# Window attention scores by tiles of 64 rows and 32 columns, q read where it was loaded, and loads cut into portions and tied to the matmuls

## The chip, the cores and the metric

One core of a Trainium2 chip runs the whole program. Its engines work side by side: PE (TensorE) multiplies matrices, DVE (VectorE) and ACT (ScalarE) do element-wise work and empty PE's result banks, POOL (GpSimd) copies and gathers, and SP (SyncE) issues most DMAs, one after the other. Each engine works through its own list of instructions in order and waits at semaphores for the others. PE writes its results to eight PSUM banks (`ps0` to `ps7`), each of 128 partitions and 512 float32 columns. PE multiplies a stationary operand, brought in by a weight load (PEld in the profile), with a moving operand that streams past it. The time is that of the device, in microseconds (us), median of several runs; lower is better.

## The reference, cut to what matters

```python
# attention, for each of 8 batches and 8 heads of 64 dimensions
s_g   = scale * q_g @ concat(k_g, k_l).T            # 32 global queries see all 32 + 512 keys
out_g = softmax(s_g) @ concat(v_g, v_l)
s_ll  = scale * q_l @ k_l.T                         # 512 local queries see keys within 32 places
s_ll  = where(abs(i - j) <= 32, s_ll, -1e9)
s_lg  = scale * q_l @ k_g.T                         # and the 32 global keys
out_l = softmax(concat(s_lg, s_ll)) @ concat(v_g, v_l)
x     = concat(out_g, out_l), heads side by side    # 8 x 544 tokens of 512 numbers
# mixture of experts: each token goes to one expert e, its own best or that of the token before it
logits = x @ w_gate                                 # 8 experts
e      = argmax(logits) or the expert of the token before, by the gate x @ w_local
out    = softmax(logits)[e] * (relu(x @ w1[e]) @ w2[e])
```

All data are float32.

## The kernel before, in words

The program has two parts. The attention fills about the first 230 us, the experts fill the rest. This case is about the attention.

A batch has four pairs of heads. One pair is one local unit (`l`): 512 queries of two heads, cut into 16 windows of 32 queries, each of which sees 128 key columns (its own window, one on either side, and the 32 global keys). Two global units (`g`), each for two pairs, compute the 32 global queries. In the function `run` the units stand in the order l, l, g, l, g, l for every batch, and one step `s` of its loop takes one unit. The step's place in the batch, `s % 6`, is called k0 to k5 below: k0, k1, k3 and k5 begin a local unit, k2 and k4 a global one.

Each step does the first half of the work for its own unit `nx` (scores, row maximum, exponent) and the second half for the unit `st` of two steps before (transposes, product with v, division by the row sums). In between, `fpiece` puts in one piece of the router's work on the finished rows: `f1` transposes a pair's output, `f2` and `f3` compute the gate's logits for a whole batch, and `f1g` and `f2g` do so for the global rows. Small router instructions on DVE are let in one at a time by `drip`.

A local unit is worked in two halves of eight windows (`hb` 0 and 1):

- `prep` copies on POOL. It spreads q of the two heads into `qbd`, where the other head's places hold zeros, and copies k with the global keys into `kx`. Both lie in rings of two buffers.
- `l_s` writes the mask into a score bank by one bf16 matmul with the identity (`idb`), and adds eight score matmuls to it. Each has 128 rows of contraction (two heads, one of them zeros) and 64 columns (32 queries of both heads), so two of them fill the bank's 128 partitions side by side.
- `l_max` takes the row maximum and subtracts it on DVE; `l_exp` is on ACT.
- `l_t` transposes the four 128 x 128 blocks of a half on PE, and ACT copies them to `pt`.
- `l_av` multiplies with v in 16 matmuls of 32 columns, four side by side, and DVE divides by the sums into `xa`, the batch's output rows.

The score banks are a ring of four, the banks for `l_av`, `g_av`, `f2`, `f2g` and a part of `f3` a ring of two (`ps_o`), and `xa` a ring of two batches. When the router has finished a batch, `f4` stores `xa` (1056 KB), `xg` and `gx` to the DRAM array `xs` through SP's list. The first `l_av` of the batch after next writes the same `xa` buffer and waits until that store has landed.

SP's list holds the loads of the attention as well: at each local step one load of q and k (`raw`, a ring of four, 528 KB) for the pair two ahead, and one of v (1040 KB, a ring of five) for the next pair. They wait only for their buffers to come free. SP waits at the head of its list, so whatever stands behind a waiting DMA waits too.

float32 matmuls appear in the profile as two records each (two passes), bf16 and fp32r ones and transposes as one.

Of the kernel before, what the change touches and what calls it, by code (L numbers as in the profile page):

```python
# [18 lines left out]
P = 128  # L19
# [16 lines left out]
NBUF = 2  # L36
# [63 lines left out]
class Attn:  # L100
    def __init__(self, tc, cst, tl, at1, at2, raw, ps, qk, qg, vw, xs):
# [13 lines left out]
        self.rs = ring(tl, [P, 2, 2, 1], F32, "rs", 3)  # L115
# [6 lines left out]
        self.pt = ring(at1, [P, 4, 2, 2, 32], F32, "pt", 4)  # L122
        self.qbd = ring(at2, [P, NW, 2, 32], F32, "qbd", NBUF)
# [4 lines left out]
        self.mask = at2.tile([P, 8, 2, 32], BF16, name="mask")  # L128
# [5 lines left out]
        self.npr = 0  # L134

    def make_mask(self):
# [8 lines left out]
        nc.vector.tensor_copy(self.mask, m0.rearrange("p (o a) k -> p o a k", o=1).broadcast_to([P, 8, 2, 32]))  # L145
        nc.vector.memset(self.mask[0:64, 0, 0, :], NEG)
        nc.vector.memset(self.mask[64:128, 7, 1, :], NEG)
# [45 lines left out]
    def prep(self, u):  # L193
# [3 lines left out]
        q = t[:, 0:SL].rearrange("p (w q) -> p w q", q=32)  # L197
        qbd, kx = u["qbd"], u["kx"] = self.qbd(), self.kx()
        k = t[:, SL:]
        kf = kx.rearrange("p m c k -> p (m c) k")  # L200
        if self.npr == 0:
            nc.scalar.copy(out=qbd[0:64, :, 0, :], in_=q[0:64])
            nc.vector.tensor_copy(qbd[64:128, :, 1, :], q[64:128])
            nc.vector.tensor_copy(kx[:, 1:8, 2, :], k[:, 32:64].rearrange("p (o k) -> p o k", o=1).broadcast_to([P, 7, 32]))
        else:
            self.cp(qbd[0:64, :, 0, :], q[0:64], [[0, NW], [0, 32]])
            self.cp(qbd[64:128, :, 1, :], q[64:128], [[0, NW], [0, 32]])
# [7 lines left out]
    def blank(self, i):  # L215
        nc = self.nc
        qbd, kx = self.qbd.t[i], self.kx.t[i]
        nc.vector.memset(qbd[0:64, :, 1, :], 0.0)
        nc.vector.memset(qbd[64:128, :, 0, :], 0.0)
        nc.vector.memset(kx[:, 0, 0], 0.0)  # L220
        nc.vector.memset(kx[:, 8, 1:3], 0.0)
# [4 lines left out]
    def l_s(self, st, hb):  # L226
        nc = self.nc
        if hb == 0:
            b, pr = st["u"]
            if pr == 0:  # L230
                self.cur[b]["xa"] = self.xa()
                self.cur[b]["xg"] = self.xg()
            st["pe"] = self.pe()
        qbd = st["qbd"]
        kf = st["kx"].rearrange("p m c k -> p (m c k)")
        sp = st["sp"] = self.bank(self.ps_s)
        mo = sp.rearrange("p t (k c) -> p t k c", c=32)[:, :, 0::3, :]
        nc.tensor.matmul(mo, self.cst.idb, self.mask[:, 4 * hb:4 * hb + 4], start=True, stop=False, skip_group_check=True)
        for t in range(4):
            for t2 in range(2):  # L240
                w = 8 * hb + 2 * t + t2
                f = 32 * (3 * (w // 2) + w % 2)
                nc.tensor.matmul(sp[64 * t2:64 * t2 + 64, t], qbd[:, w], kf[:, f:f + P], start=False, stop=True, skip_group_check=True)  # L243

    def l_max(self, st, hb):
        nc = self.nc
        mx = self.mx()
        nc.vector.tensor_reduce(out=mx, in_=st["sp"], axis=AX.X, op=ALU.max)  # L248
        self.drip()
        nc.vector.tensor_tensor(out=st["pe"][:, 4 * hb:4 * hb + 4], in0=st["sp"], in1=mx.broadcast_to([P, 4, P]), op=ALU.subtract)  # L250

    def l_exp(self, st, hb):
        pe = st["pe"][:, 4 * hb:4 * hb + 4]
        self.nc.scalar.activation(out=pe, in_=pe, func=AF.Exp, scale=SCALE)  # L254

    def l_t(self, st, hb):
        nc = self.nc
        tp = self.bank(self.ps_t)
        for i in range(4):
            nc.tensor.transpose(tp[:, i], st["pe"][:, 4 * hb + i], self.cst.idf)  # L260
        pt = self.pt()
        nc.scalar.copy(out=pt.rearrange("p i t h q -> p i (t h q)"), in_=tp)  # L262
        st["pts"] = st.get("pts", []) + [pt]

    def l_av(self, st, hb):
# [4 lines left out]
        pt = st["pts"][hb]  # L270
        o = self.ps_o()[:, 0:2 * VW].rearrange("p (g h c) -> p g h c", h=2, c=D + 1)
        for g in range(2):
            for h in range(2):
                for w4 in range(4):
                    w = 8 * hb + 4 * g + w4
                    nc.tensor.matmul(o[32 * w4:32 * w4 + 32, g, h], pt[:, 2 * g + w4 // 2, w4 % 2, h, :],  # L276
                                     v[:, w, h * (D + 1):(h + 1) * (D + 1)], start=True, stop=True, skip_group_check=True)
        rs = self.rs()
        nc.vector.tensor_scalar(out=rs, in0=o[:, :, :, D:D + 1], scalar1=1e-9, scalar2=None, op0=ALU.add)
# [3 lines left out]
        xo = c["xa"][:, 2 * hb:2 * hb + 2, 2 * D * pr:2 * D * (pr + 1)].rearrange("p g (h c) -> p g h c", c=D)  # L283
        nc.vector.tensor_tensor(out=xo, in0=o[:, :, :, 0:D], in1=rs.broadcast_to([P, 2, 2, D]), op=ALU.mult)
# [1290 lines left out]
```

## Time and profile before

| what | value |
|---|---|
| median of three runs | 690.67 us (690.36 to 690.69) |
| the profiled execution: time, span | 694.06 us, 692.3 us |
| mean granted TensorE clock | 0.995 |
| PE busy | 670.5 us, 97% of the span |
| weight loads (PEld) | 561.1 us |
| DVE busy | 426.2 us |
| ACT busy | 342.9 us |
| POOL busy | 207.7 us |
| DMA | 151.44 MB, mean 219 GB/s |

How to read it: "busy" of an engine is time in which at least one of its instructions runs. A group of instructions is named by its line in the kernel, the engine and the tiles it writes and reads (`ps<-kx,qbd` writes a PSUM bank from `kx` and `qbd`). The ends of matmuls are modelled, and consecutive ones overlap, so a matmul's duration is a latency; its cost is the distance from its start to the next start. The timeline merges equal instructions that follow one another into one row, with the start of the first.

### The profile page before, as it was taken

What the parts mean: (1) busy time and instruction counts of PE and PEld (TensorE: products, weight loads), DVE (VectorE), ACT (ScalarE), POOL (GpSimd) and SP (SyncE); (2) the same over time, 40 slices, a digit from 0 to 9 for tenths busy, and PEclk for the clock granted to TensorE, in tenths of its full rate; (3) what the DMA queues carried; (4) which work ended last, traced back from release to release, by engine and by line L of the source; (5) the groups of instructions that cost most, each with busy time, mean ns of one, the idle gap of its engine ahead of it and who ended that gap; (6) DMA issues with size and microseconds to landing.
All of it is one profiled execution on the core that took longest, in us unless ns stands there. A gap on an engine that the chain in (4) does not pass through costs nothing.

```text
span 692.3 us, 18408 instructions
## 1 busy us (share of the span) xinstructions
PE 670.5 (97%) x7253; PEld 561.1 (81%) x7253; DVE 426.2 (62%) x1050; ACT 342.9 (50%) x614; POOL 207.7 (30%) x342
## 2 busy tenths in 40 slices
PE   9999999999989899998998999999999999999995
PEld 7777777777767787897887988889898889888994
DVE  7878677688887777995517535335354516255572
ACT  4555556555455674653326625344444325255553
POOL 7634334343674301033013303040404020133023
PEclk9999999999999999999999999999999999999999
DMA  8956957866856497777418647337475417265673
GB/s 318 405 220 233 346 193 309 310 248 231 299 196 273 147 356 243 260 243 245 174 60 308 232 149 239 102 117 235 145 225 191 140 61 231 66 222 193 212 270 103
DMA packets 43011, 151.44 MB, mean 219 GB/s; under 512 B 7965, under 2 KB 9245, under 8 KB 38688
## 3 DMA queue, kind: packets, MB, share of 16 engines
q1 hardware_dynamic: 35536, 126.92, 51.6%
q0 software_dynamic: 6960, 21.90, 9.5%
q8 instruction: 77, 1.26, 0.7%
q14 instruction: 150, 1.23, 0.6%
q10 hardware_dynamic: 288, 0.13, 0.1%
HBM read 130.55 MB, written 19.69 MB: 217 GB/s over the span
## 4 chain that ended last, share of the span: by engine, by line
PE 60%; DVE 3%; issue 1%; ACT 0%; POOL 0%; POOLq 0%; DVEq 0%; ACTq 0%
PE ps L1267 29%; PE ps L1256 27%; PE ps L1210 3%; DVE wq L1165 1%; DVE wp L1165 1%; PE ps L1004 0%; PE ps L1379 0%; DVE xl L1165 0%; DVE xT L994 0%; POOL xa L1196 0%; DVE xT L996 0%; POOLq L1427 0%; DVE wp L1213 0%; PE ps L276 0%; DVE wq L1371 0%
## 5 line engine op out<-in xcount | busy, mean ns | idle before, releaser
L1273 POOL DMA_INDIRECT out_dram<-y,tk x39 | 40.4, 1036 | 317.6 <-ACT y L1272 246.3
L1267 PE MATMUL ps<-wp,wq 128*128 128x512 f32 x504 | 128.4, 402 | 1.0 <-ACT wq L1370 1.0
L1267 PEld LDWEIGHTS ps<-wp,wq 128*128 128x128 f32 x504 | 93.5, 190 | 21.1 <-ACT wq L1370 1.2
L1256 PE MATMUL ps<-wp,wp 128*128 128x256 f32 (+5 forms) x672 | 109.3, 322 | 0.2 <-issue 0.2
L1256 PEld LDWEIGHTS ps<-wp,wp 128*128 128x128 f32 x672 | 103.6, 188 | 5.3 <-issue 0.4
L1259 DVE SCALAR_TENSOR_TENSOR wq<-ps,wq 128x256 fp32r<-128x256 f32 (+5 forms) x80 | 41.7, 525 | 72.8 <-ACT wq L1258 62.6
L1213 DVE TENSOR_TENSOR wp<-ps,wp 128x512 fp32r<-128x512 f32 x40 | 27.5, 691 | 78.9 <-ACT wp L1212 78.8
L1258 ACT ACTIVATE wq<-ps 128x256 fp32r<-128x256 f32 (+5 forms) x80 | 37.3, 468 | 78.3 <-PE ps L1256 68.8
L191 POOL TENSOR_SCALAR_AFFINE_SELECT qbd<-raw 64x512 f32<-64x512 f32 x62 | 44.4, 716 | 103.3 <-PE ps L243 85.5
L243 PE MATMUL ps<-kx,qbd 128*64 128x128 f32 x1024 | 71.3, 280 | 0.2 <-issue 0.2
L1272 ACT ACTIVATE y<-ps,pp 128x512 f32<-128x512 f32 x39 | 26.9, 690 | 77.7 <-PE ps L1267 71.1
L243 PEld LDWEIGHTS ps<-kx,qbd 128*64 128x64 f32 x1024 | 55.1, 137 | 12.2 <-issue 7.8
L248 DVE TENSOR_REDUCE mx<-ps 128x4 f32<-128x512 f32 x64 | 43.9, 687 | 29.9 <-PE ps L243 29.9
L1165 DVE TENSOR_TENSOR wp<-raw,wp 128x1024 fp32r<-128x1024 f32 x47 | 57.0, 1217 | 2.8 <-ACT wp L1155 2.8
L254 ACT ACTIVATE pe<-pe 128x512 f32<-128x512 f32 x64 | 40.7, 637 | 31.7 <-DVE pe L250 31.7
L1196 POOL DMA_INDIRECT xa<-xs,idx x42 | 50.9, 1212 | 17.1 <-issue 9.4
L1155 ACT CAST wp<-raw 128x1024 fp32r<-128x1024 f32 x49 | 50.8, 1047 | 0.8 <-ACT hh L1258 0.5
L1212 ACT CAST wp<-ps 128x512 fp32r<-128x512 f32 x40 | 23.4, 590 | 53.9 <-PE ps L1210 53.3
L250 DVE TENSOR_TENSOR pe<-ps,mx 128x512 f32<-128x512 f32 x64 | 44.0, 688 | 1.6
L276 PEld LDWEIGHTS ps<-v,pt 128*32 128x32 f32 x2048 | 33.4, 110 | 13.1 <-issue 7.3
L276 PE MATMUL ps<-v,pt 128*32 128x65 f32 x2048 | 42.8, 222 | 1.1 <-issue 0.4
L262 ACT COPY pt<-ps 128x512 f32<-128x512 f32 x64 | 34.9, 610 | 17.6 <-PE ps L260 17.6
(280 smaller groups left out, 1183.3 us busy)
## 6 DMA issues: line engine op xcount, KB each, us to landing
raw<-in_w_dram SPq DMA_DIRECT2D x78, 512.0 KB, 4.1
v<-in_vw_dram SPq DMA_DIRECT2D x32, 1040.0 KB, 9.8
raw<-in_qk_dram SPq DMA_DIRECT2D x32, 528.0 KB, 8.2
xa<-in_w_dram SPq DMA_DIRECT2D x26, 512.0 KB, 5.2
xT<-in_w_dram SPq DMA_DIRECT2D x20, 512.0 KB, 3.5
xs<-xa SPq DMA_DIRECT2D x8, 1056.0 KB, 4.9
qgb<-in_qg_dram SPq DMA_DIRECT2D x8, 128.0 KB, 3.5
xa<-xs,idx POOLq DMA_INDIRECT x42
```

The lines of the kernel that those rows point to most:

```text
L191: self.nc.gpsimd.affine_select(out=out, in_=in_, pattern=pat, compare_op=ALU.is_ge, fill=0.0, base=0, channel_multiplier=0)
L243: nc.tensor.matmul(sp[64 * t2:64 * t2 + 64, t], qbd[:, w], kf[:, f:f + P], start=False, stop=True, skip_group_check=True)
L248: nc.vector.tensor_reduce(out=mx, in_=st["sp"], axis=AX.X, op=ALU.max)
L250: nc.vector.tensor_tensor(out=st["pe"][:, 4 * hb:4 * hb + 4], in0=st["sp"], in1=mx.broadcast_to([P, 4, P]), op=ALU.subtract)
L254: self.nc.scalar.activation(out=pe, in_=pe, func=AF.Exp, scale=SCALE)
L276: nc.tensor.matmul(o[32 * w4:32 * w4 + 32, g, h], pt[:, 2 * g + w4 // 2, w4 % 2, h, :], v[:, w, h * (D + 1):(h + 1) * (D + 1)], start=True ...
L1155: nc.scalar.copy(out=hi, in_=raw)
L1165: (nc.gpsimd if pool else nc.vector).tensor_tensor(out=lo, in0=raw, in1=hi.bitcast(F32), op=ALU.subtract)
L1196: self.nc.gpsimd.indirect_dma_start(out=self.xr[j] if k == "early" else self.xr4[:, j], out_offset=None, in_=src, in_offset=bass.IndirectO ...
L1256: nc.tensor.matmul(ph, a[:, dc, fs], b_[:, dc, n0:n1], start=(n == 0), stop=(n == 11))
L1259: nc.vector.scalar_tensor_tensor(out=hl[:, fc, n0:n1], in0=ph, scalar=0.0, in1=hh[:, fc, n0:n1].bitcast(F32), op0=ALU.max, op1=ALU.subtract)
L1267: nc.tensor.matmul(py, a[:, fc, js], b_[:, fs], start=(fc == 0 and k == 0), stop=(fc == 7 and k == 2))
```

## The change

Scores are now computed for each head apart, with 64 rows of contraction and 32 columns. `qbd` is gone: q is read where the load put it, rows 0 to 63 for the first head and 64 to 127 for the second. A score bank now belongs to one head (`h` 0 or 1) and holds all 16 windows: window `4*t + w4` in partitions `32*w4` and block `t`. A unit's two masks are written one after the other, right behind the transposes (`l_m`); then come all 32 score matmuls (`l_s`), alternating between the heads, and only then the two halves of the rest, which are now heads. `g_s` makes two matmuls of 32 columns where it made one of 64. `l_av` keeps its 16 matmuls for each half, and each of its two writes to `xa` now covers all 512 queries of one head.

Loads are issued by `feed`, twice in each step and each time a part: half of a v tile (520 KB), or one q-and-k tile. `get` adds to each a wait for the matmul that was last put into PE's list (`gate`). `f4` stores `xa` in two DMAs.

```diff
-        self.qbd = ring(at2, [P, NW, 2, 32], F32, "qbd", NBUF)
...
-            self.cp(qbd[0:64, :, 0, :], q[0:64], [[0, NW], [0, 32]])
-            self.cp(qbd[64:128, :, 1, :], q[64:128], [[0, NW], [0, 32]])
...
+    def get(self, out, in_):
+        d = self.nc.sync.dma_start(out, in_)
+        if self.gate is not None:
+            self.tc.add_manual_dep(d.ins, self.gate.ins.name, mybir.DependencyInfo(mybir.DependencyClass.Sync, mybir.DependencyReason.DATA), reason="pace")
...
+    def feed(self, s, hf):
+        b, k = divmod(s, 6)
+        if k < 3:
+            if b == 0 and k < 2 and hf == 0:
+                self.load(0, 2 + k)
+            self.loadv(b, 1 + k, hf)
+            return
+        b += 1
+        if b == B:
+            return
+        if k == 4:
+            self.loadv(b, 0, hf)
+        else:
+            self.load(b, (k - 3) + hf)
+            if (k, hf) == (3, 0):
+                self.load_g(b)
...
+    def l_m(self, st):
...
+        st["sps"] = [self.bank(self.ps_s) for _ in range(2)]
+        for sp in st["sps"]:
+            mo = sp.rearrange("p t (k c) -> p t k c", c=32)[:, :, 0::3, :]
+            nc.tensor.matmul(mo, self.cst.idb, self.mask, start=True, stop=False, skip_group_check=True)
+
+    def l_s(self, st):
+        nc = self.nc
+        q, kf = st["q"], st["kx"].rearrange("p m c k -> p (m c k)")
         for t in range(4):
-            for t2 in range(2):
-                w = 8 * hb + 2 * t + t2
+            for w4 in range(4):
+                w = 4 * t + w4
                 f = 32 * (3 * (w // 2) + w % 2)
-                nc.tensor.matmul(sp[64 * t2:64 * t2 + 64, t], qbd[:, w], kf[:, f:f + P], start=False, stop=True, skip_group_check=True)
+                for h in range(2):
+                    d = slice(64 * h, 64 * h + 64)
+                    self.gate = nc.tensor.matmul(st["sps"][h][32 * w4:32 * w4 + 32, t], q[d, 32 * w:32 * w + 32], kf[d, f:f + P],
+                                                 start=False, stop=True, skip_group_check=True)
...
-        nc.sync.dma_start(self.xs[r0:r0 + 4 * P].rearrange("(t p) r -> p t r", p=P), xa)
+        for t in range(0, 4, 2):
+            nc.sync.dma_start(self.xs[r0 + t * P:r0 + t * P + 2 * P].rearrange("(t p) r -> p t r", p=P), xa[:, t:t + 2])
...
             if nl:
-                self.l_s(nx, 0)
+                self.l_m(nx)
+                self.l_s(nx)
                 self.l_max(nx, 0)
             else:
                 self.g_s(nx)
                 self.g_max(nx)
+            self.feed(s, 0)
             fpiece()
             if sl:
                 self.l_av(st, 0)
             if nl:
                 self.l_exp(nx, 0)
-                self.l_s(nx, 1)
                 self.l_max(nx, 1)
             fpiece()
...
+            self.feed(s, 1)
```

How the change moves instructions shows at three places. The first is PE's list at step k5 of the first batch, where a local unit begins and another ends. `ps_65` and `ps_66` are score banks, `ps_69` and `ps_70` banks of `l_av`. Before:

```order
L260 MATMUL ps_67<-idf,pe_139 128x128 x4
L260 MATMUL ps_68<-idf,pe_139 128x128 x4
L238 LDWEIGHTS idb
L238 MATMUL ps_65<-mask,idb 128x4x2x32
L243 MATMUL ps_65<-kx_147,qbd_145 64x128 x8
L276 MATMUL ps_69<-v_134,pt_140 32x65 x16
L238 LDWEIGHTS idb
L238 MATMUL ps_66<-mask,idb 128x4x2x32
L243 MATMUL ps_66<-kx_147,qbd_145 64x128 x8
L276 MATMUL ps_70<-v_134,pt_141 32x65 x16
```

The same place in the changed kernel, up to the first two score matmuls:

```order
L280 MATMUL ps_67<-idf,pe_139 128x128 x4
L280 MATMUL ps_68<-idf,pe_139 128x128 x4
L251 LDWEIGHTS idb
L251 MATMUL ps_65<-mask,idb 128x4x2x32
L251 LDWEIGHTS idb
L251 MATMUL ps_66<-mask,idb 128x4x2x32
L262 MATMUL ps_65<-kx_145,raw_80 32x128
L262 MATMUL ps_66<-kx_145,raw_80 32x128
```

The last two rows come sixteen times over, and then the two groups of `l_av` follow each other without scores between them.

The second place is SP's list at step k2 of the third batch, where the first batch's rows are stored. Before, with the semaphores that each row waits for (DMAHW is an earlier DMA):

```order
L178 DMA raw_80<-in_qk_dram 128x1056 [waits DMAHW3_49,Pool_49]
L188 DMA v_132<-in_vw_dram 128x2080 [waits DMAHW4_49,PE_49]
L413 DMA xs<-xa_108 128x4x528 [waits DMAHW5_49,DVE_49]
L417 DMA xs<-xg_110 32x2x64 [waits DMAHW6_49]
L417 DMA xs<-xg_110 32x2x64 [waits DMAHW7_49]
```

and in the changed kernel:

```order
L173 DMA v_132<-in_vw_dram 128x1040 [waits DMAHW6_49,PE_49]
L173 DMA v_132<-in_vw_dram 128x1040 [waits DMAHW7_49,PE_49]
L173 DMA v_133<-in_vw_dram 128x1040 [waits DMAHW0_49,PE_49]
L434 DMA xs<-xa_108 128x2x528 [waits DMAHW1_49,DVE_49]
L434 DMA xs<-xa_108 128x2x528 [waits DMAHW2_49]
L438 DMA xs<-xg_110 32x2x64 [waits DMAHW3_49]
```

The store had the v load of step k1 ahead of it; now it has half a v load of step k2 ahead of it, whose wait on PE is for the last matmul of `g_s` in that same step.

The third place is DVE's list at the same step, where `l_av` of the third batch's first pair writes into `xa_108`, in the changed kernel:

```order
L324 TENSOR_REDUCE m_128<-ps_64 128x1 [waits PE_49]
L324 TENSOR_REDUCE m_128<-ps_65 128x1 [waits PE_49]
L326 TENSOR_SCALAR nb_126<-m_128 128x1 [waits DVE_49]
L397 COPY gsb_115<-ps_69 128x32 [waits PE_49]
L297 TENSOR_SCALAR rs_122<-ps_70 128x4 [waits PE_49]
L299 RECIPROCAL rs_122<-rs_122 128x4 [waits DVE_49]
L302 TENSOR_TENSOR xa_108<-ps_70,rs_122 128x4x64 [waits DMAHW2_49,DMAHW1_49,DVE_49]
```

Its last row waits for both halves of the store; its counterpart in the kernel before (line 284) stands at the same place in DVE's list and waits for the one store.

More of the change, by code (lines that the diff above doesn't have):

```diff
@@ L134, in __init__ @@
         self.npr = 0
+        self.gate = None
     def make_mask(self):
@@ L224, in bank @@
         return r().rearrange("p (t k) -> p t k", k=P)
-    def l_s(self, st, hb):
+    def l_m(self, st):
         nc = self.nc
[L228 to L238, printed above, removed]
+        b, pr = st["u"]
+        if pr == 0:
+            self.cur[b]["xa"] = self.xa()
+            self.cur[b]["xg"] = self.xg()
+        st["pe"] = self.pe()
+        st["sps"] = [self.bank(self.ps_s) for _ in range(2)]
+        for sp in st["sps"]:
+            mo = sp.rearrange("p t (k c) -> p t k c", c=32)[:, :, 0::3, :]
+            nc.tensor.matmul(mo, self.cst.idb, self.mask, start=True, stop=False, skip_group_check=True)
@@ L259, in l_t, with l_av @@
         for i in range(4):
[L260 removed]
+            nc.tensor.transpose(tp[:, i], st["pe"][:, 4 * h + i], self.cst.idf)
         pt = self.pt()
[L262 removed]
+        nc.scalar.copy(out=pt, in_=tp)
         st["pts"] = st.get("pts", []) + [pt]
[L265 removed]
+    def l_av(self, st, h):
         nc = self.nc
@@ L269, in l_av @@
         v = c["v"][pr]
[L270 to L277, printed above, removed]
+        pt = st["pts"][h]
+        o = self.ps_o()[:, 0:4 * (D + 1)].rearrange("p (t c) -> p t c", c=D + 1)
+        for t in range(4):
+            for w4 in range(4):
+                self.gate = nc.tensor.matmul(o[32 * w4:32 * w4 + 32, t], pt[:, t, 32 * w4:32 * w4 + 32],
+                                             v[:, 4 * t + w4, h * (D + 1):(h + 1) * (D + 1)], start=True, stop=True, skip_group_check=True)
         rs = self.rs()
-        nc.vector.tensor_scalar(out=rs, in0=o[:, :, :, D:D + 1], scalar1=1e-9, scalar2=None, op0=ALU.add)
+        nc.vector.tensor_scalar(out=rs, in0=o[:, :, D:D + 1], scalar1=1e-9, scalar2=None, op0=ALU.add)
         self.drip(hold=True)
@@ L295, in g_s @@
                 k = c[("qk", pr)][:, SL:]
-                nc.tensor.matmul(sp[64 * i:64 * i + 64, 0:n1 - n0], c["qg"][:, pr], k[:, n0:n1], start=True, stop=True, skip_group_check=True)
+                for h in range(2):
+                    r = 64 * i + 32 * h
+                    self.gate = nc.tensor.matmul(sp[r:r + 32, 0:n1 - n0], c["qg"][:, pr, h], k[:, n0:n1], start=True, stop=True, skip_group_check=True)
             st["sp"].append(sp[:, 0:n1 - n0])
@@ L439, in run @@
         self.load_g(0)
-        self.loadv(*pairs[0]["u"])
+        for hf in range(2):
+            self.loadv(0, 0, hf)
         self.cst.ident()
```

66 lines of the change are left out of this document (27 added, 39 removed).

## The prediction

> **What bounds the kernel now.** I read the page's busy times first, then the busy times by stretch, one stretch for each attention batch (cut where the last scores of step k5 end), then PE's timeline of two steps, DVE's timeline of the same, and SP's.
>
> ```profile
> PE 670.5 (97%) x7253; PEld 561.1 (81%) x7253; DVE 426.2 (62%) x1050; ACT 342.9 (50%) x614; POOL 207.7 (30%) x342
> ```
> ```profile
> core 0: us, PE busy (x) PEld busy (x) DVE busy (x) ACT busy (x) POOL busy (x), PEclk, DMA share, GB/s
> 0.00:26.70 26.70, 25.11 (x414) 19.54 (x414) 21.16 (x65) 13.30 (x29) 18.78 (x70) 1.00 0.91 352
> 26.70:55.20 28.50, 28.19 (x589) 21.27 (x587) 21.86 (x81) 16.01 (x37) 11.06 (x24) 1.00 0.73 278
> 55.20:83.00 27.80, 27.80 (x591) 21.19 (x589) 21.09 (x73) 16.02 (x38) 11.07 (x24) 1.00 0.75 271
> 83.00:110.90 27.90, 27.49 (x585) 21.06 (x585) 20.81 (x69) 15.73 (x37) 11.06 (x24) 1.00 0.73 270
> 110.90:139.10 28.20, 28.20 (x601) 21.42 (x597) 21.57 (x78) 16.30 (x38) 11.06 (x24) 1.00 0.80 292
> 139.10:167.40 28.30, 27.94 (x593) 21.17 (x594) 22.40 (x83) 16.16 (x39) 11.07 (x24) 1.00 0.61 230
> 167.40:200.00 32.60, 30.79 (x616) 23.06 (x614) 27.35 (x94) 15.75 (x38) 23.13 (x45) 1.00 0.67 238
> 200.00:231.00 31.00, 29.98 (x619) 23.02 (x617) 24.12 (x81) 17.98 (x39) 13.24 (x24) 1.00 0.72 272
> ```
>
> Batches 1 to 5 (second to sixth row; batches count from 0) are PE's: it is busy for all of their 28 us. DVE is at 21 to 22 of 28, so a faster PE can win 6 to 7 us there before DVE is full. In the two last batches, where the router's work comes on top, DVE has 27.35 and 24.12 us. The experts behind 231 us are not touched, so all gain or loss lies in these eight rows. Next, PE in one local step (k5) and in steps k1 to k3:
>
> ```profile
> 118.68 0.33 PE L359 MATMUL ps<-idf,xg 128*128 128x128 f32 x1
> 118.94 0.66 PE L276 MATMUL ps<-v,pt 128*32 128x65 f32 x32
> ...
> 121.37 1.09 PE L260 MATMUL ps<-idf,pe 128*128 128x128 f32 x8
> 122.39 1.14 PE L296 MATMUL ps<-raw,qgb 128*64 128x256 f32 x8
> 123.46 0.27 PE L375 MATMUL ps<-xgT,wgg 128*32 128x32 f32 x8
> 123.54 0.64 PE L276 MATMUL ps<-v,pt 128*32 128x65 f32 x32
> 124.12 0.65 PE L352 MATMUL ps<-idf,xa 128*128 128x128 f32 x4
> 124.70 0.67 PE L276 MATMUL ps<-v,pt 128*32 128x65 f32 x32
> 125.30 1.09 PE L260 MATMUL ps<-idf,pe 128*128 128x128 f32 x8
> ...
> 134.26 0.89 PE L339 MATMUL ps<-v,ptg 128*32 128x65 f32 x48
> 135.09 1.10 PE L260 MATMUL ps<-idf,pe 128*128 128x128 f32 x8
> 136.02 0.27 PE L238 MATMUL ps<-mask,idb 128*128 128x256 bf16 x1
> 136.22 1.09 PE L243 MATMUL ps<-kx,qbd 128*64 128x128 f32 x16
> 137.24 0.67 PE L276 MATMUL ps<-v,pt 128*32 128x65 f32 x32
> 137.84 0.28 PE L238 MATMUL ps<-mask,idb 128*128 128x256 bf16 x1
> 138.05 1.09 PE L243 MATMUL ps<-kx,qbd 128*64 128x128 f32 x16
> 139.08 0.66 PE L276 MATMUL ps<-v,pt 128*32 128x65 f32 x32
> 139.67 0.87 PE L328 MATMUL ps<-idf,pg 128*128 128x128 f32 x6
> 140.38 0.27 PE L238 MATMUL ps<-mask,idb 128*128 128x256 bf16 x1
> ```
>
> From start to next start: a mask 0.21 us, a half of scores 1.02, transposes of a local unit 0.93, `l_av` 0.60, `g_t` 0.71, `g_s` 1.07, `g_av` 0.83, one `f1` 0.58, `f1g` 0.26.
>
> **PE's part: the scores.** Sixteen score records lie on two column tiles, so eight rounds; the 32 records of `l_av` on four, also eight rounds. Rounds of 128 and of 65 columns cost 1.02 and 0.60 us, so a column costs (1.02 - 0.60) / (8 x 63) = 0.83 ns, a score round 107 ns, and 0.17 us is left for filling and emptying the array at a change of tile shape. After the change a pair has 64 records on eight tiles. No row shows two row tiles at work together. If all eight run side by side as the four of `l_av` do, that is again eight rounds, 1.02 us for the whole pair; if the two row halves take turns, sixteen rounds, 1.88. I take 1.02: four tiles of `l_av` already take a record every 0.60 / 32 = 18.8 ns, filling included, and each head has a bank of its own. The second mask costs 0.04 to 0.21 us behind the first (without or with the 0.17); I take 0.10. So masks and scores of a pair go from 2 x 1.23 = 2.46 to 1.33 us. Two `l_av` in a row at k1 and k5, and `g_s`, `f2g`, `l_av` in one shape at k2, spare a change of shape each, at most 0.17, taken as 0.15. `g_s` itself keeps its four rounds. Sum for a batch: 4 x 1.13 + 3 x 0.15 = 5.0 us less for PE, 27.8 to 22.8, if nobody makes it wait.
>
> The Trainium skill, "TensorE: Matmul & The Clock Gate" (section "Wait — 56ns, not 53.3ns?"), says that start-to-start of matmuls never drops below about 25 ns however short they are. By it 64 records would take at least 1.6 us. The 18.8 ns above are below that already, so for column tiles the trace disagrees; for row tiles no run here shows it, and it stays a rival.
>
> **POOL and the start.** The q copies go, two of 717 ns for each pair on POOL, and in the first steps four DVE memsets and a copy:
>
> ```profile
> L191 POOL TENSOR_SCALAR_AFFINE_SELECT qbd<-raw x62: 710/717/737, 5.9 to 218.9; 64x512 f32<-64x512 f32 x62
> L218 DVE MEMSET qbd<- x2: 485/485/485, 1.7 to 5.8; 64x512 f32 x2
> ```
>
> POOL has 11 of 28 us in a batch, so its 1.4 us for a pair are worth nothing. On DVE 4 x 0.49 us lie in the first batch. The loads move too. Issue and landing of them before:
>
> ```profile
> v<-in_vw_dram SPq DMA_DIRECT2D x32, 1040.0 KB, 9.8
> raw<-in_qk_dram SPq DMA_DIRECT2D x32, 528.0 KB, 8.2
> ```
>
> Now a q-and-k tile is issued two or more steps before `prep` needs it (some 8 us), v in halves three or more before `l_av`, with less in flight at a time. I put that at nothing, covered by this lead; without it, PE would wait for the missing part of 8 us.
>
> **DVE, who is late next.** DVE's work in a step stays, but its start moves: PE issues all scores and both `l_av` in 2.1 us, and DVE needs two halves for them.
>
> ```profile
> 137.36 0.69 DVE L248 TENSOR_REDUCE mx<-ps 128x4 f32<-128x512 f32 x1 [1.42 <-PE ps L243]
> ...
> 139.43 0.68 DVE L248 TENSOR_REDUCE mx<-ps 128x4 f32<-128x512 f32 x1
> ...
> 141.52 0.41 DVE L284 TENSOR_TENSOR xa<-ps,rs 128x256 f32<-128x256 f32 x1
> ```
>
> One half is 2.07 us, and the second `xa` write ends 4.57 us after the first maximum begins, which is 0.12 after PE's next group. Set 0 at the end of the scores in k5. DVE has `xa` at 4.7. PE: two `l_av` 1.05, `g_t` 0.71, masks 0.31, scores 1.02: at 3.1 it wants `xa` for `f1` of k0, all of it now, since each write covers one head. It waits 1.6. Then `f1`, `g_av`, transposes, masks, scores: k1's scores end at 8.4. DVE's k1 runs from 8.5 to 13.1, and the first `l_av` of k2, whose bank the second of k1 has, could begin at 11.9: 1.2 of waiting. From there PE runs through k2, k3 and k4 with little waiting (the four slower router pieces let DVE catch up) and ends the scores of k5 at about 25.8. So of 5.0 us some 3 come back as waits, and a batch of 27.8 becomes 25.8; DVE is idle for 25.8 - 21.1 = 4.7 us of it.
>
> **SP, the new wait.** The `gate` makes SP wait at each load for PE, and the store of `xa` stands behind such a load.
>
> ```profile
> 119.55 0.38 SPq L413 DMA_DIRECT2D xs<-xa  x1
> ```
> ```profile
> 125.81 0.42 DVE L284 TENSOR_TENSOR xa<-ps,rs 128x256 f32<-128x256 f32 x1 [1.12 <-DMA xs<-xa]
> ```
> ```profile
> xs<-xa SPq DMA_DIRECT2D x8, 1056.0 KB, 4.9
> ```
>
> Before, the store left during k1 (119.55) as soon as the router had written the last of `xa`, and DVE's first `xa` write of k2 still waited 1.12 us for it, 6.2 us after the issue. Now it leaves only when `g_s` of k2 is through: at 8.4 + 0.26 + 1.05 + 1.02 + 1.05 = 11.8 on the clock above, plus 0.4 for half a v load. Landing: 4.9 (median) at the least, 6.2 plus 2.4 for half a v tile ahead (half of 4.9, by size) at the most, so 17.1 to 20.8; I take 18.0, since the 1.12 row is the nearest and the half tile may overlap. DVE would have been ready at 14. Behind the waiting DVE stand all its work of k2 and k3, and behind that PE's `f2` (bank) and `f1` of k4: 0.4 to end the write, 0.75 for the second, 4.7 for k3 with the logits, 0.2 for semaphores, then PE 0.5 + 0.83 + 0.93 + 0.31 + 1.02, together 9.7. The batch takes 27.7 (26.8 to 30.5): as long as before. This holds in batches 2 to 5; the earlier ones have no store, and in the last two the router runs faster and the store leaves at k5.
>
> **Sum.** With DVE's idle 4.7 us added to its busy time: batch 0, 21.2 - 2.0 + 4.7 = 23.9 against 26.7, 2.8 less; batch 1, 25.8 to 26.6 against 28.5, 2.3 less; batches 2 to 5, 0; batch 6, 27.35 plus 1.5 to 4.7 (the router fills gaps) against 32.6, 2.2 less; batch 7, 28.8 against 31.0, 2.2 less. The tail begins with DVE later by what it lags, at most 1, taken as 0.5. Together 9.0 us. The profiled execution took 694.06 us (span 692.3, 1.8 around it), 3.4 over the median; 9.0 off it is 685.1, off the median 690.67 it is 681.7.
>
> **Rivals.**
> 1. The store costs nothing (it lands before DVE needs `xa`, or DVE's lag is greater): batches 2 to 5 win 2 us each, 674. For it: the wait was only 1.12 us before, and the split may land sooner. Against: the issue moves back by some 3 us relative to k1.
> 2. The row halves do not run side by side. With 1.88 us for a pair, the 0.86 more lie on PE's path at k1, k3 and k5 in a batch without store (25.8 + 2.6) and at k1 and k5 in one with it (27.7 + 1.7): batches 0, 1, 6 and 7 end about level, 2 to 5 lose 1.5 each: 697, slower. It decides from the point where the gain is gone: 9.0 us over 4 x 2 + 4 x 3 = 20 score groups on the path is 0.45 us for a pair, that is a record every (1.02 + 0.45 - 0.17) / 64 = 20.3 ns instead of 13.3. For it: no row shows row tiles. Against: the four column tiles show no loss. A floor of 25 ns for a start would give (1.6 + 0.17 - 1.02) x 20 = 15 us more than forecast, 697; that is the rule of the Trainium skill cited above.
> 3. The store lands at the late end, 20.8: batches 2 to 5 lose 2.5 each, 691, no change.
>
> **How the numbers follow.** Forecast 0.47 (676 to 686), rival 1 0.27, rival 2 0.15, rival 3 0.11. The range goes from 669 (rival 1 with fewer waits for DVE) to 694 (rival 3, and part of rival 2). A change within 0.2% (1.4 us) cannot be told from none here. Faster: 0.47 + 0.27 + some of rival 3, 0.77; same 0.08; slower 0.15.
>
> **What would show it.** Scores and masks of a pair in 1.3 us on PE, 64 records in one group; 1.9 is rival 2. Batches 0 and 1 shorter by 2 to 3 us, batches 2 to 5 as before, with DVE's first `xa` write of k2 waiting 3 to 4 us for the store and PE's `f2` behind it; no such wait is rival 1. PE idle at `f1` of k0 and at the first `l_av` of k2, released by DVE. The forecast is wrong if PE's idle time in a batch is well under 3 us, or if some load is late and PE or POOL waits for it, which I put at nothing.

## The result and the profile after

The changed kernel takes 719.61 us (median of four runs, 718.07 to 725.23), the kernel before 690.68 on the same chip (690.36 to 691.48): a ratio of 1.043, 95% interval 1.038 to 1.049. It is slower by 29 us, where 681.7 had been forecast. The profiled execution after has a time of 718.07 and a span of 716.3 us, at a mean granted TensorE clock of 0.973 (0.995 before).

First the busy times of the page, after. PE has 1152 records more than before and is busy for 20 us less, while the span grew by 24: PE waits now.

```profile
PE 650.3 (91%) x8405; PEld 541.7 (76%) x8405; DVE 417.8 (58%) x1045; ACT 342.9 (48%) x613; POOL 165.5 (23%) x280
```

The busy times by stretch, after, one row for each attention batch, cut in the same way as those of before:

```profile
core 0: us, PE busy (x) PEld busy (x) DVE busy (x) ACT busy (x) POOL busy (x), PEclk, DMA share, GB/s
0.00:26.70 26.70, 21.62 (x526) 16.38 (x526) 16.61 (x53) 12.43 (x27) 13.25 (x63) 0.94 0.92 331
26.70:53.30 26.60, 24.12 (x750) 18.12 (x731) 20.81 (x80) 15.77 (x36) 5.52 (x17) 1.00 0.81 250
53.30:85.00 31.70, 26.10 (x748) 18.76 (x731) 20.21 (x72) 15.92 (x37) 5.42 (x16) 0.95 0.77 247
85.00:117.40 32.40, 25.66 (x747) 19.23 (x731) 20.45 (x72) 16.28 (x37) 5.38 (x17) 0.95 0.75 242
117.40:151.30 33.90, 26.17 (x750) 19.38 (x732) 20.93 (x72) 16.01 (x37) 5.43 (x17) 0.90 0.75 231
151.30:185.40 34.10, 25.56 (x749) 19.07 (x732) 21.46 (x81) 15.60 (x38) 5.40 (x17) 0.90 0.72 228
185.40:219.90 34.50, 29.47 (x778) 21.36 (x760) 27.03 (x96) 16.21 (x38) 17.69 (x38) 0.90 0.76 238
219.90:251.40 31.50, 26.05 (x777) 19.52 (x761) 23.25 (x84) 17.31 (x39) 6.83 (x14) 1.00 0.77 254
```

The attention ends at 251.4 us in place of 230.8, and 20.6 us of the loss lie in these rows: +0.2, -1.9, +3.9, +4.1, +6.1, +5.8, +1.9, +0.5. (For this the batches of before end at 26.5, 55.0, 82.8, 111.1, 138.9, 167.2, 199.8 and 230.8; the rows in the prediction lie 0.2 us off.) The batches with a store to wait for (2 to 5) lose most. The clock column shows a third thing that before did not have: 0.90 to 0.95 in six of the eight rows, in place of 1.00.

PE's waits after, longest sums first. The fourth word is what was waited for; "issue" is a wait for which the trace has no releaser:

```profile
PE ps L387 <- DVE xa L302: 13.8, 4, 5.1
PE ps L294 <- issue: 6.3, 4, 2.3
PE ps L262 <- issue: 6.3, 7, 2.9
PE ps L372 <- DVE xa L302: 4.9, 5, 1.4
PE ps L280 <- issue: 3.6, 2, 2.2
PE ps L316 <- issue: 3.3, 2, 2.7
```

The first row is `f2` of batches 2 to 5. In the attention the issue waits come to 20.1 us in 16 waits; before they were 0.9 us in 3. Now the store, on SP and then on DVE, in batch 4:

```profile
122.52 9.70 SPq L173 DMA_DIRECT2D v<-in_vw_dram  x5
132.31 0.90 SPq L434 DMA_DIRECT2D xs<-xa  x2
```
```profile
132.81 0.18 DVE L299 RECIPROCAL rs<-rs 128x4 f32<-128x4 f32 x1
140.10 0.42 DVE L302 TENSOR_TENSOR xa<-ps,rs 128x256 f32<-128x256 f32 x1 [7.11 <-DMA xs<-xa]
```

Five halves of v, each behind its matmul, hold the store until 132.31, and DVE stands still for 7.11 us, in all four batches together 27.3 (before: 1.12 in the row shown in the prediction). And PE, around `f1` of k0 and at `f2`, with the scores between:

```profile
120.97 0.38 PE L251 MATMUL ps<-mask,idb 128*128 128x256 bf16 x2
121.29 1.16 PE L262 MATMUL ps<-kx,raw 64*32 64x128 f32 x64
122.37 0.66 PE L372 MATMUL ps<-idf,xa 128*128 128x128 f32 x4
...
140.58 1.94 PE L387 MATMUL ps<-xT,wgl 128*32 128x512 f32 x8 [4.73 <-DVE xa L302]
142.29 1.09 PE L294 MATMUL ps<-v,pt 128*32 128x65 f32 x32
```

Masks and scores of a pair take 0.32 + 1.08 = 1.40 us to the next start: all eight tiles do run side by side. After the wait of 4.73 us, `f2` takes 1.71 us and `l_av` 1.02 to the next start (0.89 and 0.60 before): PE comes back at a lower clock: the granted clock is 0.50 from 138.62 to 145.45, and 1.00 on either side.

```profile
138.62:145.45 6.83, 4.87 (x78) 2.90 (x78) 4.21 (x11) 1.12 (x2) 1.31 (x4) 0.50 0.59 183
```

### The profile page after: what moved, and what is told of

The parts are those of the page before. It is cut to its first block, busy times and chain, and to the rows that moved or that the text cites. A ratio compares the mean times of both kernels' runs of the same rounds, so it can differ in the third digit from the quotient of the medians.

```text
span 716.3 us, 20775 instructions
## 1 busy us (share of the span) xinstructions
PE 650.3 (91%) x8405; PEld 541.7 (76%) x8405; DVE 417.8 (58%) x1045; ACT 342.9 (48%) x613; POOL 165.5 (23%) x280
## 4 chain that ended last, share of the span: by engine, by line
PE 57%; DVE 3%; ACT 1%; issue 1%; POOL 0%; POOLq 0%; DVEq 0%; ACTq 0%
PE ps L1284 27%; PE ps L1273 25%; PE ps L1227 2%; DVE wp L1182 1%; PE ps L1396 1%; DVE wq L1182 1%; PE ps L1021 0%; DVE xT L1011 0%; POOL xa L1213 0%; ACT wp L1172 0%; DVE xT L1013 0%; DVE hl L1276 0%; POOLq L1444 0%; DVE wp L1230 0%; DVE xl L1182 0%
## 5 line engine op out<-in xcount | busy, mean ns | idle before, releaser
L1290 POOL DMA_INDIRECT out_dram<-y,tk x39 | 41.9, 1075 | 316.3 <-ACT y L1289 226.1
L213 POOL TENSOR_SCALAR_AFFINE_SELECT kx<-raw 128x384 f32<-128x384 f32 (+3 forms) x127 | 43.0, 368 | 154.3 <-DMA raw<-in_qk_dram 63.8
L1213 POOL DMA_INDIRECT xa<-xs,idx x42 | 51.0, 1215 | 17.1 <-issue 9.4
L294 PEld LDWEIGHTS ps<-v,pt 128*32 128x32 f32 x2048 | 36.8, 118 | 23.5 <-issue 17.1
L294 PE MATMUL ps<-v,pt 128*32 128x65 f32 x2048 | 44.8, 235 | 9.6 <-issue 6.3
L1229 ACT CAST wp<-ps 128x512 fp32r<-128x512 f32 x40 | 23.4, 588 | 53.5 <-PE ps L1227 53.5
L262 PE MATMUL ps<-kx,raw 64*32 64x128 f32 x2048 | 40.9, 275 | 6.3 <-issue 6.3
L302 DVE TENSOR_TENSOR xa<-ps,rs 128x256 f32<-128x256 f32 x64 | 27.0, 422 | 28.5 <-DMA xs<-xa 27.3
L262 PEld LDWEIGHTS ps<-kx,raw 64*32 64x32 f32 x2048 | 29.3, 106 | 16.1 <-issue 15.1
```

Source lines behind the costliest of these rows:

```text
L213: self.nc.gpsimd.affine_select(out=out, in_=in_, pattern=pat, compare_op=ALU.is_ge, fill=0.0, base=0, channel_multiplier=0)
L262: self.gate = nc.tensor.matmul(st["sps"][h][32 * w4:32 * w4 + 32, t], q[d, 32 * w:32 * w + 32], kf[d, f:f + P], start=False, stop=True, sk ...
L294: self.gate = nc.tensor.matmul(o[32 * w4:32 * w4 + 32, t], pt[:, t, 32 * w4:32 * w4 + 32], v[:, 4 * t + w4, h * (D + 1):(h + 1) * (D + 1)] ...
L1213: self.nc.gpsimd.indirect_dma_start(out=self.xr[j] if k == "early" else self.xr4[:, j], out_offset=None, in_=src, in_offset=bass.IndirectO ...
L1290: sc = nc.gpsimd.indirect_dma_start(out=self.out, out_offset=bass.IndirectOffsetOnAxis(ap=self.g[1][:, j:j + 1], axis=0), in_=y, in_offset ...
```

## The experiments

Two theories were to be told apart. Theory 1: the loss comes from the gate, which holds the store of `xa`. Theory 2: it comes from the 64 records for a pair, which PE's instruction supply does not keep up with. Ratios are to the kernel before on the same chip. "Issue waits" are PE's in the attention.

| kernel | time, us | ratio (95%) | attention ends | issue waits, us |
|---|---|---|---|---|
| before | 690.68 | | 230.8 | 0.9 |
| after | 719.61 | 1.043 (1.038 to 1.049) | 251.4 | 20.1 |
| e1, one half of v not gated | 723.84 | 1.040 (1.035 to 1.044) | 260.5 | 26.6 |
| e3, new scores, old loads | 717.84 | 1.031 (1.025 to 1.037) | 247.6 | 29.0 |
| e4, old scores, new loads | 719.75 | 1.036 (1.032 to 1.039) | 252.7 | 1.4 |
| e5, half the score records | 702.49 | 1.011 (1.007 to 1.014) | 238.4 | 2.9 |
| e6, half the records, old loads | 686.65 | 0.993 (0.990 to 0.996) | 225.7 | 6.5 |
| e7, old scores, portions, no gate | 693.72 | 1.003 (1.001 to 1.005) | 230.4 | 1.1 |
| e8, new scores, few loads | (724.15) | | 227.7 | 10.9 |
| e9, before with 64 records | 705.89 | 1.022 (1.018 to 1.026) | 243.3 | 10.9 |
| e10, after without the gate | 719.26 | 1.034 (1.031 to 1.036) | 252.1 | 28.3 |
| h2, third pair new | 702.44 | 1.011 (1.007 to 1.015) | 236.3 | 8.5 |
| h0, first pair new | 702.00 | 1.008 (1.005 to 1.011) | 233.8 | 8.8 |
| h02, first and third pair new | 707.50 | 1.016 (1.013 to 1.019) | 242.3 | 15.6 |
| m1, masks behind the transposes | 694.57 | 0.998 (0.996 to 0.999) | 228.8 | 1.5 |
| m2, and one group of scores | 698.88 | 1.005 (1.002 to 1.007) | 233.6 | 1.3 |

The chips differ, so runs are compared by what each takes over the kernel before on its own chip. e8 works on old data, so only its attention counts. The kernel before took 695.42 beside e1 to e5, 692.08 beside e6 to e9, 696.00 beside e10 and the h runs, 696.03 beside the m runs.

**e1: one gated half freed.**

```diff
     def feed(self, s, hf):
         b, k = divmod(s, 6)
+        if (k, hf) == (2, 0):
+            self.gate = None
```

> The changed kernel, with one wait less: the first v half that SP issues in step k2, ahead of the store of xa, no longer waits for PE's g_s of k2. Theory 1 (the late store is the loss): the store's issue moves ahead by 3 us or more, DVE's wait for it at the first xa write of k2 (27.3 us in 4 waits after the change) shrinks below 8 us in all, PE's wait at f2 (13.8 us in 4) goes, and batches 2 to 5 come from 31.7 to 34.1 us down to some 27, as batch 1 has it (26.6): about 695 us. Theory 2 (PE's own issue stalls, some 20 us that the trace puts down to no releaser): the stalls stay, batches 2 to 5 lose no more than 2 us each: 712 or more. If both hold: about 700, with the stalls at issue still there. What is left against 690.7 then is not the store's.

SP's queue in batch 4 of this kernel:

```profile
127.24 7.50 SPq L173 DMA_DIRECT2D v<-in_vw_dram  x5
134.83 1.01 SPq L436 DMA_DIRECT2D xs<-xa  x2
```

The wait for the store stayed (28.4 us in 4 waits), so the run does not tell the theories apart: the expectation was wrong about what holds the store. Of the five halves ahead of it the last but one is gated by k1's second `l_av`, which ends some 2 us before `g_s`; freeing only the last half moves the store's issue by no more than that. Nor did the earlier issue bring an earlier landing:

```profile
145.23 0.42 DVE L304 TENSOR_TENSOR xa<-ps,rs 128x256 f32<-128x256 f32 x1 [7.88 <-DMA xs<-xa]
```

The store was issued 1.0 us before `g_s` ended (at about 135.78; 0.7 after it in the changed kernel), and DVE went on 9.5 us after that end, in place of 8.4. The store's first packet left 4.3 us after the issue (2.9 in the changed kernel, 0.9 before), behind packets of v. So the halves of v, let through shortly before, hold the store in the DMA queue as well as in SP's list.

**e3 and e4: scores alone, loads alone.** e3 takes the loads of the kernel before with the new scores; e4 takes `qbd`, masks, `l_s`, `l_av` and `g_s` of the kernel before with `feed`, `get` and the split store of the changed one.

> The new scores, masks and heads, with the loads as they were before: whole v tiles, issued at the local steps, no gate, one store. Theory 1 (gate and store are the loss): the scores give what the prediction gave them where no store stands in the way, 2.0 to 2.8 us a batch in all eight batches: 672 to 678 us. Theory 2 (PE stalls at issue because of its many short records): PE still shows some 20 us of issue waits in the attention, and the time is 688 to 695, no better than before. A third way, late q and k tiles, would show as POOL waiting on raw and PE on kx.

> The old scores and masks (q copies on POOL, both heads in a bank), with the changed loads: portions, gate, store in two pieces behind the gated half. Theory 1: the store leaves after g_s of k2 as in the changed kernel, DVE and PE's f2 wait for it, batches 2 to 5 lose 3 to 5 us each: 703 to 711 us. Theory 2 (the scores' many records are the loss): no record is added, so 690 to 693 us, no issue waits on PE.

e4 shows theory 1 by itself. DVE's wait for the store and the stretches of batches 1 and 4 in it:

```profile
DVE xa L307 <- DMA xs<-xa: 26.6, 8, 6.2
```
```profile
26.50:54.40 27.90, 27.83 (x592) 21.17 (x587) 21.40 (x84) 16.08 (x37) 11.87 (x27) 1.00 0.77 243
120.30:154.30 34.00, 30.19 (x591) 22.43 (x589) 21.05 (x73) 16.10 (x38) 11.06 (x24) 0.90 0.74 229
```

Batch 1 has no store to wait for and keeps its length; batch 4 is 6.2 us longer than before, with the old scores, 1.4 us of issue waits in all and the clock at 0.90. The forecast of 703 to 711 was too low for the same reason as the prediction: the price of a late store was put too low.

e3 shows theory 2 by itself: no gate, yet 717.8, far above the 688 to 695 that its expectation gave for this theory. PE in batch 4 of e3:

```profile
127.16 0.65 PE L357 MATMUL ps<-v,ptg 128*32 128x65 f32 x29
130.40 0.53 PE L357 MATMUL ps<-v,ptg 128*32 128x65 f32 x19 [2.59 <-issue]
130.86 1.35 PE L278 MATMUL ps<-idf,pe 128*128 128x128 f32 x8
132.01 0.63 PE L249 MATMUL ps<-mask,idb 128*128 128x256 bf16 x2
132.57 1.75 PE L260 MATMUL ps<-kx,raw 64*32 64x128 f32 x56
```

PE stops for 2.59 us in the middle of a group, 29 of its 48 records done, and the trace has no releaser. The records behind it are slow: the granted clock is 0.50 from 131.55 to 134.96. The two parts of the change cost 24 and 22 us, but together only 29. The issue waits are 20.1 us with the store's wait and 29.0 without: it fits that PE's supply catches up while PE waits for the store, though no record shows this directly.

**e5 and e6: half the score records.**

```diff
-                for h in range(2):
+                for h in range(1):
...
-        mx, sp = self.mx(), st["sps"][h]
+        mx, sp = self.mx(), st["sps"][0]
```

> The changed kernel with the score matmuls of head 1 left out (32 in place of 64 records for a pair, still eight rounds on four tiles); both maxima read head 0's bank, so head 1's scores are not computed. Loads, gate and store are those of the change. Theory 1 (store): the wait at the store and f2 stays, 714 to 720 us. Theory 2 (PE's instruction supply): PE has 1024 records fewer, the issue waits go from some 20 us to under 5, and the time falls by 10 us or more, to 700 to 710.

> Head 1's score matmuls left out (its scores are not computed) and the loads as they were before: both suspected costs away at once, PE's rounds as in the changed kernel. If the loss consists of just these two (records that outrun their supply, and the store behind the gated v halves), batches 1 to 5 take about 25.8 us, as the prediction had them without a store wait, and the attention ends at 215 to 222 us (230.8 before): 674 to 682 us. If the loads of before are too late for the faster PE (a third cause), batches stay at 28 or more, with POOL waiting for raw: 690 or more.

e5, with loads and gate as in the change, loses most of its issue waits (2.9 us) and 21 us of its time (702.5 beside 723.8 of e1 on the same chip), and keeps the wait for the store (25.7 us); so the issue waits go with the records, not with the gate. e6 has neither cost and is the only kernel with the new tiles that beats before, but by 5.4 us, not by the 10 to 18 expected. Its batches 2 and 5 have 25.7 and 26.4 us, near the forecast's 25.8; batches 1, 3 and 4 have 27.4 to 29.1, with 2.4 and 3.3 us of issue waits in two of them; batch 6 has 35.2.

**e7: is it the gate or the portions?**

```diff
-        if self.gate is not None:
+        if False:
```

> The old scores, with the loads in portions and the store in two pieces at their new places, and no gate: SP waits only for free buffers. Theory 1 (the gate delays the store): the store leaves as soon as the router has written xa, the wait for it falls from 26.6 us to about that of before, batches 2 to 5 go from 33.5 to 28 us: 690 to 694. Rival (the portions themselves, more loads ahead of the store in SP's queue and in the DMA queues): the wait stays, 705 or more.

The portions with the old scores, without the gate. The wait of the `xa` writes for the store, in the view of that line:

```profile
  DMA xs<-xa: 0.4, 1
```

0.4 us in place of 26.6, and 1.6 us over the kernel before in place of 24.3. With the old scores the gate is the cause; the portions and the split store by themselves cost at most half a per cent.

**e8: do the loads starve the supply?**

```diff
-    def get(self, out, in_):
+    def get(self, out, in_, b=0):
+        if b >= 2:
+            return
```

> The new scores with the loads at their old places, but those of batches 2 to 7 left out (the tiles keep what the first batches brought, so the attention of six batches is computed on old data, and the router's choice and the experts' work may differ; it is read by its attention part alone). All 64 records for a pair stay. If the instruction fetches wait behind the loads' packets, PE's issue waits vanish from batch 2 on and these batches fall from some 31.5 to some 26 us. If the fetch has a round trip of its own that short bursts outrun, the issue waits stay at 2 to 4 us a batch, and the batches fall by less than 2 us.

Batches 3 to 5 of e8, and under them the same three of e3, which has the loads:

```profile
84.60:110.70 26.10, 23.47 (x754) 18.05 (x735) 20.38 (x72) 15.98 (x38) 5.60 (x17) 1.00 0.16 53
110.70:136.70 26.00, 23.36 (x748) 18.02 (x731) 20.39 (x72) 15.96 (x37) 5.48 (x17) 1.00 0.17 54
136.70:163.30 26.60, 23.69 (x750) 17.97 (x731) 21.41 (x81) 15.65 (x38) 5.51 (x17) 1.00 0.15 52
```
```profile
90.00:121.90 31.90, 25.98 (x751) 19.60 (x732) 20.66 (x72) 16.23 (x37) 5.50 (x17) 0.95 0.68 246
121.90:152.10 30.20, 25.37 (x747) 19.14 (x731) 20.55 (x72) 16.26 (x37) 5.43 (x17) 0.94 0.70 249
152.10:181.40 29.30, 24.53 (x751) 18.24 (x732) 21.87 (x81) 16.18 (x38) 5.54 (x17) 1.00 0.69 251
```

Same score records, same order, and with the DMA share at 0.16 in place of 0.69 the issue waits of batches 2 to 6 fall from 18.5 us to 1.3 (they are 0 in batches 3 to 5), the clock stays at 1.00 and the batch takes 26. So the records alone do not stall PE: they stall it when the loads run too.

The trace's DMA records show what it waits for. Packets of 16,384 bytes of the kind "instruction" stand on a queue of their own, 77 before and 87 after, ten more for PE's 1152 records more. In e3, five of its longest stops beside the packet nearest to each (us; the end of the last record before the stop is modelled):

```
PE stops   packet begins   packet ends   PE goes on
  16.78        16.73          17.68         19.07
  29.18        28.80          29.82         31.23
  77.55        77.25          78.20         79.57
  95.33        95.24          96.18         97.61
 127.81       128.10         129.00        130.40
```

The packet itself takes 0.9 to 1.0 us as it does in the kernel before; it begins about when PE has run out, and PE goes on 1.4 us after its end (1.3 to 1.5 in all fifteen issue waits of e3 over 0.7 us). In the attention of the kernel before, 128 PE records in a row never took less than 4.4 us; after, one such window in twenty takes 3.2 or less (ten packets for 1152 records make some 115 records a packet), so a packet that comes as late as before is now too late. That the packet comes late only beside the loads is what e8 shows; where in the DMA engines it waits, no record shows. The Trainium skill, "DMA: Bandwidth & Descriptors" (section "Queues, rings and completion order"), says that each DMA engine serves its queues in turn and takes a whole bundle of some 9 to 17 descriptors from one before it goes on. That would explain it: a load row of 8320 bytes takes 0.31 us here, so by the page's count an estimate of 2.8 to 5.3 us behind one bundle. But by it rows half as long (4160 bytes, 0.16 us) would halve the wait, and e10, which has them, has 28.3 us of issue waits beside e3's 29.0. The runs agree that the loads hold up the fetch, and do not bear out that figure.

**e9: records without row tiles.**

```diff
-                nc.tensor.matmul(sp[64 * t2:64 * t2 + 64, t], qbd[:, w], kf[:, f:f + P], start=False, stop=True, skip_group_check=True)
+                for h in range(2):
+                    nc.tensor.matmul(sp[64 * t2 + 32 * h:64 * t2 + 32 * h + 32, t], qbd[:, w, h], kf[:, f:f + P], start=False, stop=True, skip_group_check=True)
```

> The kernel before with each score matmul of 64 columns of the array cut into two of 32 (128 rows by 32 columns, four tiles side by side): the same products, twice the score records (64 for a pair), the same loads. In PE time nothing should change (four tiles take a record in half the time). If the number of records alone is what costs, PE shows issue waits as in the changed kernel and the batches grow by 2 to 3 us: 705 or more. If it is the density (the changed kernel has 128 records in as little as 2.1 to 3.3 us, the kernel before never in under 4.4), the bursts here are half as dense (64 in 2.2 us) and only few stalls show: 690 to 697.

A half of the scores now has 32 records on four tiles in no more time (0.89 us to the next start, 1.02 before), and stops appear:

```profile
85.31 1.08 PE L244 MATMUL ps<-kx,qbd 128*32 128x128 f32 x32
...
94.81 0.88 PE L261 MATMUL ps<-idf,pe 128*128 128x128 f32 x6 [1.22 <-issue]
```

13.8 us slower with nothing changed but the number of score records and their width. This fits the first reading (705 or more) in time, and lies between the two in its issue waits (10.9 us).

**e10: the change without the gate.** The edit is that of e7, made on the changed kernel.

> The whole changed kernel, only without the gate (loads in portions at their new places, SP waiting for free buffers alone). With the store's wait gone (theory 1) and all 64 records kept: the wait for the store falls from 27.3 us to under 6; if the two costs simply added up the time would be about 697. But with the old loads the same scores took 717.8, with 29 us of issue waits in the attention; if PE's starved instruction fetch takes up whatever the store leaves (theory 2), it is 710 to 718 again, with 25 to 30 us of issue waits.

The store's wait fell from 27.3 to 1.6 us, but the issue waits rose from 20.1 to 28.3. The kernel is 23.3 us over before, where the changed one is 28.9 over on another chip (the ratios' intervals do not meet). So of the 23 us that the gate costs with the old scores, taking it out of the change gives back some 5 or 6. Theory 2 had it in the main.

**h2, h0, h02: how many pairs can have the new tiles?** The kernel before, with the new masks, scores and `l_av` only for the pairs named in `NEW`.

```diff
+NEW = (2,)          # h0: (0,); h02: (0, 2)
...
+        u["new"] = pr in NEW
+        if not u["new"]:
+            qbd = u["qbd"] = self.qbd()
```

> The kernel before, but the third pair of each batch (step k3) takes its scores by tiles of 64 rows and 32 columns with q read where it was loaded, the other three as before; loads as before. PE's work in a batch falls by 1.1 us, its score records rise from 128 to 160. By the stalls of the doubled records alone (12.5 us over 32 pairs, 0.4 us a pair) 0.7 us a batch is left: 4 to 6 us less, 685 to 687, if DVE and the dense burst do not take it; if a single burst of 64 records already outruns its fetch, 690 to 698.

> As the one before, with the first pair of each batch (step k0) in place of the third: there the router piece's 48 records stand behind the scores in place of 64, and the second step's 32 old ones follow. Same sums: 685 to 687 if the fetch keeps up, 690 to 698 if not.

> First and third pair by the new tiles. PE's work falls by 2.3 us a batch, records rise from 128 to 192. With 0.4 us of stalls a pair and some waiting for DVE: 680 to 686; if the stalls grow faster than the records, as the changed kernel's 0.8 to 0.9 us a pair suggest, 688 to 700.

All three fell on the bad side, 6.0 to 11.5 us slower than before. One pair costs 8.5 or 8.8 us of issue waits, two 15.6, four (e3) 29.0: 7 to 9 us for each pair of the four, against 1.1 x 8 = 9 us of PE work saved. The clock falls too (0.985 in h2, 0.971 in e3), and the balance is negative from the first pair on.

**m1 and m2: the rest of the forecast gain.** In m1 both masks of a unit go right behind the transposes, as `l_m` does it; in m2 the second half's scores follow the first's directly.

```diff
+                self.l_m(nx)
                 self.l_s(nx, 0)
+                self.l_s(nx, 1)       # m2 alone
                 self.l_max(nx, 0)
...
-                self.l_s(nx, 1)       # m2 alone
```

> The kernel before with one part of the change alone: the masks of both halves right behind the transposes of the step, in one group, ahead of the scores; score matmuls (32 records a pair), order of the rest and loads as before. After the change the two masks took 0.31 us to the next start against 2 x 0.21 before. If that is a saving of its own, PE wins 0.1 us a pair, and the second half's scores follow l_av without a mask between: 3 to 5 us over 32 pairs, 0.4 to 0.7%. If DVE or the banks, both taken at once now, eat it: within 0.2%.

> As the one before, and both halves of the scores in one group (32 records in 2.0 us) ahead of both l_av, as the changed kernel has them, still with 32 records for a pair of 64 columns each. By the forecast's 0.15 us for a change of shape, 2 to 5 us less than the run with the masks alone, about 1% less than before in all. If the groups win nothing (the first l_av starts a microsecond later, and DVE gets two halves at once): as the masks alone. Records are as dense as before at most 32 in 1 us, so no issue waits on either view.

m1 wins 0.2% (0.998, interval 0.996 to 0.999): 2.0 us in the attention of the profiled executions, where 0.1 us for each of 32 pairs would be 3.2. Beside e6, which leaves work out, it is the only kernel that beats the one before, by little. m2 loses half a per cent, which neither view had. Its scores in one group:

```profile
126.15 1.97 PE L247 MATMUL ps<-kx,qbd 128*64 128x128 f32 x32
```

1.89 us to the next start in place of 2 x 1.02, so the group does save a change of shape. But its batches 1 to 4 are 27.6 to 28.5 us, against 27.4 to 28.2 of m1, and batch 6, where the router's lists come on top, takes 36.2 against 32.6. Whether that long batch 6 comes from the one group stays open: the changed kernel, e3 and e6, which have the group, show 34.5, 33.9 and 35.2 there, but e5 and e10, which have it too, 31.8 and 32.5.

## Why the prediction was wrong, point by point

- **Scores and masks of a pair, 2.46 to 1.33 us: right.** 1.40 measured, 64 records in 1.08 us, one every 16.9 ns, so rival 2 (the row halves take turns) did not happen. The floor of 25 ns of the Trainium skill, "TensorE: Matmul & The Clock Gate" (section "Wait — 56ns, not 53.3ns?"), does not hold for tiles of 64 rows and 32 columns side by side: the trace disagrees.
- **"If nobody makes it wait", 25.8 us for a batch without store: right where it applies.** e8's batches 3 to 5, with neither loads nor late store, take 26.0 to 26.6, with 2.6 to 2.8 us of waits for DVE and ACT (some 2.8 had been forecast), among them the two at `f1` of k0 (1.2 to 1.3) and at the first `l_av` of k2 (1.1), where the prediction had put 1.6 and 1.2.
- **The first step that failed: nothing in the prediction asked how fast PE gets its instructions.** The step from "64 records on eight tiles" to "again eight rounds" counted rounds and not records. The records cost 20.1 us of issue waits after the change (29.0 by themselves). No row of before showed a price: its issue waits were 0.9 us. It showed a bound that went unused, 128 records never in under 4.4 us. And the loads, which the prediction asked only whether they come in time themselves, are what makes the fetch late (e8).
- **The second: the store's landing, taken at 18.0 on the clock of the prediction (17.1 to 20.8).** The mechanism and its place were right: DVE waits at the first `xa` write of k2, PE's `f2` behind it, in batches 2 to 5. The size was too small. In batch 4 `g_s` ends at about 131.65 and DVE goes on at 140.10, 8.4 us later, where 6.2 had been taken and 9.0 was the late end. By the prediction's own chain such a landing makes a batch of 29.9; 33.9 was measured, of which 2.9 are issue waits and 2.8 the clock (next point). The store's first packet leaves 2.9 us after its issue (0.9 before), behind the halves of v that the gate had let through just before; the half tile that "may overlap" did not overlap. By e4 and e7 the gate costs some 23 us on the old scores (24.3 over before with it, 1.6 without).
- **The third: the clock was taken as 1.00.** Batch 4 has 750 records and PE busy for 26.2 us at a granted 0.90 after the change; e8's has 748 and 23.4 at 1.00. So the waits cost some 2.8 us more than their length there. Batch 4 closes by it: 26.2 busy, 4.7 for the store and 2.9 at issue make 33.8 of the 33.9. The Trainium skill, "TensorE: Matmul & The Clock Gate" (section "Part 1: The HAM clock gate (the "warmup" mystery)") says that PE falls to half its clock after an idle window of about 3.4 us. Behind a stop of 4.73 us the trace shows half the clock, from 2.8 us into the stop on (`f2` in 1.71 us, 0.89 before). But in e3 it shows half the clock behind a stop of 2.59 us too, so here a shorter stop was enough.
- **Batches 0, 1, 6 and 7, 2.2 to 2.8 us less each: wrong but for batch 1** (1.9 less). Issue waits took batch 0 (2.3 us) and batch 7 (4.0). Batch 6 lost 1.9, of which only 1.2 are issue waits. Its row has a granted clock of 0.90 (half from 196.65 to 203.48, worth up to 3.4 us), with no wait of PE over 0.6 us in the ten before; what started it stays open.
- **The tail, 0.5 us:** the rest of the program takes 464.9 us against 461.5, 3.4 more in these two executions; this was not taken apart.
- **The rivals.** Rival 3, a late landing, had the right place and direction, but at 691 it was far too small: the changed loads alone (e4) cost 24.3 us. The case that came, a rate of PE's instructions as the limit, was not among them.

## What to carry to other kernels

Count instructions as well as array time: a tile scheme that does the scores in half the rounds with twice the records asks more of PE's instruction supply, and where loads keep the DMA engines at 0.7, a kernel with one window of 128 records in twenty at 3.2 us or less was too fast (20.1 to 29.0 us of stops), and one with none under 4.4 was not (0.9). Whether the densest bursts or the mean rate decide, the runs do not separate. Before a wait is added to a queue that works in order, list everything that stands behind it: here the store behind five gated loads cost some 23 us by itself. And price a long wait of PE above its length: here the records behind it ran at half the clock for some 5 us.

## What the runs showed of the hardware that was not expected

- Tiles of 64 rows and 32 columns on both row halves and all four column groups work at the same time: 64 float32 records of 128 columns in 1.08 us.
- PE stops in the middle of a group for up to 3.2 us (h02) when its instruction packet (16 KB, 0.9 to 1.0 us) is late. The stops grow with the records (0.9, 8.5, 15.6, 29.0 us with 0, 1, 2 and 4 of four pairs cut into 64) and go with the loads (18.5 to 1.3 us in batches 2 to 6).
- The two costs do not add up: 24 and 22 us alone, 29 together. Taking out the gate left 23.3 us over before (e10), taking out half the score records 7.1 (e5); only with both out was the kernel faster than before, by 5.4 us (e6).
